# Block-sparse attention with a gated projection: some gathers put behind value products, and new schedule tables

## The chip, the cores and the metric

The kernel runs on one core of one Trainium2 chip. The metric is the device time of one execution in microseconds (us). The engines are named as the profile names them: PE (TensorE, with PEld for its weight loads), DVE (VectorE), ACT (ScalarE), POOL (GpSimd) and SP (SyncE, which here only issues DMAs).

## The reference

```python
def _attn_ref(q, k, v, sampled_blocks):          # q, k, v: (4, 8, 768, 64); sampled_blocks: (24, 3)
    scores = scale * np.matmul(q, k.transpose(0, 1, 3, 2))
    ...
    mask = np.abs(blk_i - blk_j) <= window       # blocks of 32 rows, window 1
    mask = mask | (blk_i == 0) | (blk_j == 0) | (blk_i == n_blocks - 1) | (blk_j == n_blocks - 1)
    for qb in range(n_blocks):
        for kb in sampled_blocks[qb]:
            mask[qb * block:(qb + 1) * block, kb * block:(kb + 1) * block] = True
    ...                                          # softmax over the allowed keys
    return np.matmul(attn, v)

def _moe_ref(x, w_val, conv_w, w_out):           # x: (4, 768, 512)
    gate_pre[t] = sum over k < 5 of conv_w[k] * xp[t + k]      # causal convolution along the rows
    gate = 1.0 / (1.0 + np.exp(-gate_pre))
    return gate * (x @ w_val) @ w_out
```

The attention's output, heads side by side, is `x` of the second part.

## The kernel before, in words

**Units.** The 24 query blocks of a batch are worked in pairs of neighbours: 11 ordinary pairs, and one pair of the first and the last block, which see all keys (the global pair; `GLOB_AT` says at which place of the batch it comes). An ordinary pair is one unit, the global pair two, so four batches make 52 units, numbered 0 to 51 here. An ordinary unit has its keys in a tile `kg` (a ring of 4): the first and last block, its own pair, the neighbours, and three sampled blocks for each query block. Its values are in two tiles: `va` (ring of 3) by plain DMAs, and `vb` (3 buffers) by two **gathers**, indirect DMAs that GpSimd issues, one for each query block, with row numbers from `idx`.

**Steps.** The program is one loop over steps n. In step n stand, on each engine in the order of the program: loads of keys and values for units ahead, the scaling of `qc` (two units ahead), the scores `sc` of unit n (`s` for a global unit) with maxima `mx` on DVE and exponentials `pe` on ACT, the copies of keys for unit n + 2, the value products `av` of unit n - 2, the transposes `pt` of unit n - 1 with their evictions `ptr`, and `finish` of unit n - 3 (transposes `xp`, evictions `xT`). On PE the order is thus sc(n), av(n - 2), pt(n - 1), xp(n - 3). A value block is 64 matmuls of 128x65 in the trace (48 where batches 0 and 1 take `va` in one wide piece, 96 for a global unit).

**Fills.** Between the two halves of `pt`, and after them, `fill` puts pieces of the second part: `vp` (x @ w_val, 12 matmuls) or half an `op` (times w_out, 6 matmuls), as many as the table `FILLS` says for that half step. `prepare` does pieces of the weights' decoding, of the gate (`th` on DVE and ACT) and of splitting x into a high and a low part (`xh` on ACT, `xl` on POOL), by `STEPS`. After `vp`, DVE makes `y`, ACT its high part `yh`, POOL the low part `yl`; `op` needs both. No fill can run until all weights are decoded and the first rows are ready, which is in step 23. `V_AT`, `K_AT` and `WEIGHTS_AT` say when the loads of values for the global pair (`vn`), of the next batch's keys (`k`) and of weights (`wst`) are issued.

**Order.** Each engine's instructions are kept in the program's order (the helper `InOrder`, whose line all recorded instructions have in the profile, so that rows are told apart by tile). A gather waits for its `vb` buffer, which the value products of three pairs earlier read. In the kernel before, gathers are issued in `load_values`, at the head of step n, before the scaling and the copies of keys, and their buffer is free after av(n - 3), which stands in step n - 1.

Of the kernel before, what the change touches and what calls it, by code (L numbers as in the profile page):

```python
# [11 lines left out]
AF = mybir.ActivationFunctionType  # L12
ALU = mybir.AluOpType
AX = mybir.AxisListType
SP, POOL, ACT = mybir.EngineType.SP, mybir.EngineType.Pool, mybir.EngineType.Activation

B, H, S, D = 4, 8, 768, 64
BLK, NB, NR = 32, 24, 3
# [8 lines left out]
PAIRS = [(2 * p + 1, 2 * p + 2) for p in range(NP - 1)]  # L27
RING = 4
VRING = 3
GLOB_AT = (6, 3, 5, 4)  # L30
V_AT = ((3, 5, 6), (1, 1, 4), (2, 3, 6), (5, 6, 7))
K_AT = ((11, 11, 11), (6, 6, 10), (9, 10, 10), (8, 9, 9))
LAG_T, LAG_V, LAG_X = 1, 2, 3
WEIGHTS_AT = (2, 5, 5, 6, 7, 10, 11, 17)
DECODE_LAG = 2
SCALE_AHEAD = 2
COPY_AHEAD = 2
WIDE, SPLIT = 2, 4

COPY_ON = ("PPPAAA", "PPPSSS", "SSSSSS", "SSSSSS")  # L40
Q_ON = "AAAP"
OWN_ON = ("PP", "PP", "AP", "PP")
LOW_ON = "PPPPPVPP"
OPENING = 34

SP_VALUES = ((), (), (), ())
REGS = 4

FILLS = (
    "11213202124222020022203013"  # L50
    "23432111131112010111111112"
    "01021101111120110111011101"
    "11111101212001120021110201"
    "112110"
)
STEPS = (
    "22010020122222323311322110"
    "10321201212212221224323113"
    "22311202102131332232122210"
    "13342500120220021004344321"  # L60
    "212011"
)
STEPS_TAIL = 1

# [2 lines left out]
def attention_moe(ctx, tc, qb, kb, v, ve, sampled, w_val, conv_w, w_out, ident_in, slot_in, out):  # L67
# [236 lines left out]

    def block_numbers(pr, eng):

        mine = [n for n in range(2 * NR) if {"P": POOL, "A": ACT, "S": SP}[COPY_ON[pr.bt.b][n]] == eng]
        if not mine:
            return
        assert mine == list(range(mine[0], mine[0] + len(mine)))  # L310
        first = NR * PAIRS[pr.p][0] + mine[0]
        _, regs = nc.values_load_multi_w_load_instructions(
            sm[0:1, first : first + len(mine)], engines=[eng], min_val=0, max_val=NB - 1,
            skip_runtime_bounds_check_because="block numbers are drawn from [0, 24)",
        )
        for n, reg in zip(mine, regs):
            yield 5 + 4 * (n // NR) + n % NR, reg

    def load_keys(pr):
# [13 lines left out]
        for place, reg in block_numbers(pr, SP):  # L333
            sp.dma_start(pr.kg[:, place, :], kb[:, b, bass.ds(reg, 1), :].rearrange("p o x -> p (o x)"))

    def copy_keys(pr):
        if pr.glob:
            return
        bt, kt, i0 = pr.bt, pr.kg, PAIRS[pr.p][0]
        assert bt.loaded >= 3  # L340
        if pr.seq:
            numbers = {eng: list(block_numbers(pr, eng)) for eng in (POOL, ACT)}
# [4 lines left out]
        for eng, copy in ((POOL, pool.tensor_copy), (ACT, act.copy)):  # L347
# [7 lines left out]
    def load_values(pr):  # L355
        b = pr.bt.b
        if pr.glob:
            return
        if pr.p == 0 and b:
            indices(b)  # L360
        if pr.p == 0 and SP_VALUES[b]:
            block_rows(b)
        vt = va[pr.seq % VRING]
        pr.va = vt
        if pr.p < VRING:
            sp.dma_start(vt[0 : 2 * BLK, :], ve[b])
        i0 = PAIRS[pr.p][0]
        sp.dma_start(vt[64:128, :], v[b * S + i0 * BLK : b * S + (i0 + 2) * BLK, :])
        pr.vb = three.tile([128, 2, H * DV], F32, tag="vb", name="vb")
        for j, i in enumerate(PAIRS[pr.p]):  # L370
            if j in SP_VALUES[b]:
                near = i + (1 if j else -1)
                near = (b * NB + near if 0 < near < NB - 1 else B * NB) * BLK
                sp.dma_start(pr.vb[0:BLK, j, :], v[near : near + BLK, :])
                if pr.p % REGS == 0:
                    held[j] = nc.values_load_multi_w_load_instructions(
                        sv[0:1, b, j, pr.p : min(pr.p + REGS, NP - 1), :].rearrange("p i r -> p (i r)"), engines=[SP],
                        min_val=0, max_val=B * NB,
                        skip_runtime_bounds_check_because="block numbers are drawn from [0, 24)",
                    )[1]  # L380
# [19 lines left out]
    for pr in pairs:  # L400
        for e in range(2 if pr.glob else 1):
            un = Unit()
            un.pr, un.e = pr, e
            un.last = not pr.glob or e == 1
            units.append(un)

# [62 lines left out]

    def transposes(un):  # L470
        un.PT = []
        for p in un.P:
            turn[0] += 1
            pt = (bank("pt", ps_pt, "pt") if turn[0] % 2 else ps_pt.tile([128, 512], F32, tag="pt", name="pt"))
            pt = pt.rearrange("p (c s) -> p c s", c=4)
            for c in range(4):
                transpose(pt[:, c, :], p[:, 128 * c : 128 * c + 128], ident)
            t = three.tile([128, 4, 128], F32, tag="ptr", name="ptr")
            act.copy(t, pt)
            un.PT += [t[:, c, :] for c in range(4)]  # L480
            yield

    def values(un):
# [3 lines left out]
        if pr.glob:  # L487
            assert pr.bt.loaded == 6
            pr.bt.valued += 1
            for h in range(2):  # L490
                for c in range(6):
                    pt = un.PT[4 * h + c if c < 4 else 4 + 2 * h + c]
                    for hp in range(HP):
                        cols = slice(BLK * hp, BLK * hp + BLK)
                        hd = 2 * hp + h
                        matmul(
                            pr.av[cols, un.e, h, :], pt[:, cols], pr.bt.vn[:, c, hd * DV : (hd + 1) * DV],
                            start=c == 0, stop=c == 5, tile_position=(0, BLK * hp),
                        )
        else:  # L500
# [8 lines left out]
            for a, h, b, hd in slots:  # L509
                for c in range(1 if wide else 0, 2):  # L510
                    for j in range(2):
                        rows = slice(64 * b + BLK * j, 64 * b + BLK * j + BLK)
                        vt = pr.vb[:, j, :] if c else pr.va
                        matmul(
                            pr.av[rows, a, h, :], un.PT[4 * h + 2 * a + c][:, rows], vt[:, hd : hd + DV],
                            start=c == 0, stop=a + h == 2 if wide else c == 1, tile_position=(0, rows.start),
                        )
# [9 lines left out]
    def finish(pr):  # L527
        if pr.p == 0:
            if pr.bt.b >= 2:

# [10 lines left out]
        xv = xp[:, 0:2, :].rearrange("p j (c s) -> p c j s", c=CH)  # L541
        if pr.glob:
            for e, s0 in ((0, 0), (1, S - BLK)):
                act.copy(xT[:, :, o + s0 : o + s0 + BLK], xv[:, :, e, :])
        else:
            s0 = o + PAIRS[pr.p][0] * BLK
            act.copy(xT[:, :, s0 : s0 + 2 * BLK], xp[:, 0:2, :].rearrange("p a (b s) -> p (a b) s", b=2))


    class Rows:  # L550
# [190 lines left out]
    for n in range(N + LAG_X):  # L741
# [5 lines left out]
        def more_values():  # L747
            return more("values", freed(n - LAG_V - 1) + VRING, load_values)

        if n == 0:  # L750
            more_keys()
            numbers_first = {eng: list(block_numbers(pairs[0], eng)) for eng in (POOL, ACT)}
            until("scaled", 0, scale)
            indices(0)
            until("copied", 0, copy_keys)
# [17 lines left out]
        if n == 0:  # L773
            while more_keys() or more_values():
                more_values()
        if 0 <= n - LAG_V < N:
            values(units[n - LAG_V])
        if 0 <= n - LAG_T < N:
            for half, _ in enumerate(transposes(units[n - LAG_T])):
                at_half = 2 * n + min(half, 1)  # L780
# [4 lines left out]
            prepare(int(STEPS[2 * n]))  # L785
        if 0 <= n - LAG_X < N and units[n - LAG_X].last:
            pr = units[n - LAG_X].pr
            finish(pr)
# [61 lines left out]
```

## Time and profile before

| what | value |
| --- | --- |
| median of 3 runs | 396.49 us (396.42, 399.18, 396.49) |
| the profiled execution: its time, its span | 398.18 us, 396.1 us |
| PE busy | 362.1 us of the span (91%) |
| DVE, ACT, POOL busy | 240.6, 256.4, 226.9 us |
| DMA | 72.36 MB, mean 183 GB/s |

Busy time of PE holds matmuls that overlap one another and that are drawn out by late operands, so 91% isn't 91% of its peak. Columns are explained where rows stand, below.

### The profile page before, as it was taken

What the parts mean: (1) busy time and instruction counts of PE and PEld (TensorE: products, weight loads), DVE (VectorE), ACT (ScalarE), POOL (GpSimd) and SP (SyncE); (2) the same over time, 40 slices, a digit from 0 to 9 for tenths busy, and PEclk for the clock granted to TensorE, in tenths of its full rate; (3) what the DMA queues carried; (4) which work ended last, traced back from release to release, by engine and by line L of the source; (5) the groups of instructions that cost most, each with busy time, mean ns of one, the idle gap of its engine ahead of it and who ended that gap; (6) DMA issues with size and microseconds to landing.
All of it is one profiled execution on the core that took longest, in us unless ns stands there. A gap on an engine that the chain in (4) does not pass through costs nothing.

```text
span 396.1 us, 15575 instructions
## 1 busy us (share of the span) xinstructions
PE 362.1 (91%) x6308; PEld 283.6 (72%) x6308; DVE 240.6 (61%) x523; ACT 256.4 (65%) x620; POOL 226.9 (57%) x330
## 2 busy tenths in 40 slices
PE   8689878897989999899989998999999999999995
PEld 8366555664667876679567885788678867989894
DVE  4345576567699687465684962695655566734920
ACT  1856788766798676667666776676485666553521
POOL 0874754874498856735653286854862773172640
PEclk9969999999999999999999999999999999999999
DMA  7986797999636877786546375897544434001102
GB/s 231 317 287 203 220 299 226 265 268 309 177 114 194 227 224 216 241 256 193 166 132 243 91 211 150 269 305 236 137 117 149 117 94 152 28 27 54 53 28 80
DMA packets 52439, 72.36 MB, mean 183 GB/s; under 512 B 6928, under 2 KB 34448, under 8 KB 52368
## 3 DMA queue, kind: packets, MB, share of 16 engines
q1 hardware_dynamic: 44896, 47.82, 39.8%
q0 software_dynamic: 7040, 23.43, 19.6%
q8 instruction: 50, 0.82, 0.9%
q14 instruction: 21, 0.17, 0.1%
q10 hardware_dynamic: 432, 0.11, 0.1%
HBM read 65.05 MB, written 6.29 MB: 180 GB/s over the span
## 4 chain that ended last, share of the span: by engine, by line
PE 72%; ACT 8%; DVE 6%; issue 6%; DMA 4%; POOL 1%; another core or an unknown queue 1%; SPq 0%; ACTq 0%; POOLq 0%; DVEq 0%
PE vp L85 17%; PE av L85 15%; PE op L85 14%; PE pt L85 11%; PE sc L85 10%; DVE mx L85 3%; PE s L85 3%; ACT ptr L85 2%; PE xp L85 2%; DMA k<-in_k 2%; ACT pe L85 2%; DMA vb<-in_v,idx 2%; POOL yl L85 1%; ACT th L85 1%
## 5 line engine op out<-in xcount | busy, mean ns | idle before, releaser
L85 POOL DMA_INDIRECT vb<-in_v,idx x88 | 88.7, 1008 | 45.8 <-PE av L85 24.0
L85 DVE SCALAR_TENSOR_TENSOR th<-xT,cw,th 128x384 f32<-128x384 f32 x128 | 91.0, 721 | 14.9 <-ACT th L85 11.3
L85 ACT ACTIVATE pe<-sc,mx 128x256 f32<-128x256 f32 x176 | 69.2, 481 | 42.0 <-DVE mx L85 39.2
L85 DVE TENSOR_REDUCE mx<-sc 128x2 f32<-128x512 f32 x88 | 56.6, 684 | 55.3 <-PE sc L85 42.2
L85 ACT COPY ptr<-pt 128x512 f32<-128x512 f32 x112 | 64.7, 602 | 20.2 <-PE pt L85 9.5
L85 POOL TENSOR_TENSOR yl<-y,yh 128x384 fp32r<-128x384 f32 x32 | 33.5, 1050 | 69.1 <-ACT yh L85 68.8
L85 PE MATMUL sc<-kg,qc 64*32 64x256 f32 x1408 | 57.1, 388 | 3.9 <-issue 1.3
L85 POOL COPY kg<-k 128x256 f32<-128x256 f32 (+1 forms) x154 | 50.4, 367 | 9.2 <-DMA k<-in_k 9.0
L85 PEld LDWEIGHTS av<-va,ptr 128*32 128x32 f32 (+1 forms) x1056 | 33.6, 119 | 27.9 <-issue 15.1
L85 PE MATMUL op<-wo,yh 128*128 128x512 f32 x192 | 53.1, 398 | 0.1
L85 PE MATMUL vp<-xh,wv 128*128 128x384 f32 x256 | 51.8, 344 | 0.4 <-ACT ptr L85 0.4
L85 PE MATMUL pt<-ident,pe 128*128 128x128 f32 x352 | 51.4, 283 | 0.4 <-ACT rest L85 0.4
L85 PE MATMUL av<-vb,ptr 128*32 128x65 f32 x1408 | 44.6, 224 | 7.8 <-issue 7.3
L85 PE MATMUL av<-va,ptr 128*32 128x65 f32 (+1 forms) x1056 | 45.4, 228 | 6.9 <-issue 4.1
L85 PEld LDWEIGHTS vp<-xh,wv 128*128 128x128 f32 x256 | 43.8, 188 | 0.9 <-ACT ptr L85 0.7
L85 PEld LDWEIGHTS pt<-ident,pe 128*128 128x128 f32 x352 | 39.1, 142 | 6.8 <-ACT rest L85 1.0
L85 POOL TENSOR_TENSOR xl<-xT,xh 128x384 fp32r<-128x384 f32 x32 | 35.4, 1114 | 12.7 <-ACT xh L85 12.5
L85 PEld LDWEIGHTS av<-vb,ptr 128*32 128x32 f32 x1408 | 33.6, 111 | 12.0 <-issue 9.8
L85 PEld LDWEIGHTS sc<-kg,qc 64*32 64x32 f32 x1408 | 25.8, 107 | 22.0 <-issue 13.4
L85 PEld LDWEIGHTS op<-wo,yh 128*128 128x128 f32 x192 | 35.0, 188 | 7.2 <-ACT yh L85 0.5
L85 PE MATMUL op<-wo,yl 128*128 128x512 f32 x96 | 31.8, 410 | 0.9 <-POOL yl L85 0.7
L85 ACT CAST yh<-y 128x384 fp32r<-128x384 f32 x32 | 16.8, 526 | 20.5 <-DVE y L85 17.0
(72 smaller groups left out, 461.5 us busy)
## 6 DMA issues: line engine op xcount, KB each, us to landing
kg<-in_k SPq DMA_DIRECT2D x165, 64.0 KB
vn<-in_v SPq DMA_DIRECT2D x12, 520.0 KB
qc<-in_q SPq DMA_DIRECT2D x48, 128.0 KB
k<-in_k SPq DMA_DIRECT2D x12, 512.0 KB
out<-ot SPq DMA_DIRECT2D x24, 256.0 KB
va<-in_v SPq DMA_DIRECT2D x44, 130.0 KB
wst<-in_w_val SPq DMA_DIRECT2D x4, 512.0 KB
wst<-in_w_out SPq DMA_DIRECT2D x4, 512.0 KB
```

The lines of the kernel that those rows point to most:

```text
L85: made = getattr(self.eng, name)(*args, **kwargs)
```

## The change

The gathers are no longer issued in `load_values`: they are put on a list `waiting`, and `gather` issues all that is on it. A letter for each step in the new table `GATHER` says where. S: at the head of the step, as before (also steps 0 to 2). U: after av(n - 2) in POOL's order, with no wait of its own. G: there too, and the gather waits until the last matmul of av(n - 2) has ended (`un.done`). W: the values of one pair more are loaded behind av(n - 2), with no added wait. Of 56 letters 25 are S, 24 G, 5 U and 2 W; G stands at steps 4 to 8, 10, 15, 18, 26 to 28, 31 to 36, 38 to 41 and 53 to 55, U at 1 to 3, 17 and 37, W at 43 and 44. The steps that follow a global pair by three and four have no gather to issue in either kernel.

Other parts: `Q_ON` moves the scaling of `qc` in batch 2 from ACT and in batch 3 from POOL to DVE (12 each). `PTR_ON` and `XT_ON` move 7 of 112 `ptr` evictions and 7 of 52 `xT` evictions from ACT to DVE. `LOW_ON` moves one weight chunk's low part from DVE to POOL and another the other way. `OPENING` is 31 matmuls instead of 34. The global pair of batch 1 comes one place later. `FILLS` and `STEPS` have new numbers throughout.

`OWN_ON` names DVE for some of a pair's own keys. It is read as `OWN_ON[b]` in `copy_keys`, where `b` is not the pair's batch but the enclosing function's last loop value, 3, in both kernels; its entry is "PP" before and after, so in the built programs POOL copies these keys in both, and DVE has no `kg` copy in either.

```diff
-GLOB_AT = (6, 3, 5, 4)
-V_AT = ((3, 5, 6), (1, 1, 4), (2, 3, 6), (5, 6, 7))
-K_AT = ((11, 11, 11), (6, 6, 10), (9, 10, 10), (8, 9, 9))
+GLOB_AT = (6, 4, 5, 4)
+V_AT = ((2, 5, 8), (0, 0, 7), (0, 0, 4), (3, 5, 6))
+K_AT = ((10, 11, 11), (7, 8, 11), (3, 8, 11), (3, 4, 9))
-WEIGHTS_AT = (2, 5, 5, 6, 7, 10, 11, 17)
+WEIGHTS_AT = (0, 5, 5, 5, 5, 7, 12, 15)
-Q_ON = "AAAP"
-OWN_ON = ("PP", "PP", "AP", "PP")
-LOW_ON = "PPPPPVPP"
-OPENING = 34
+Q_ON = "AAVV"
+OWN_ON = ("VP", "DP", "AD", "PP")
+LOW_ON = "PVPPPPPP"
+OPENING = 31
...
+GATHER = "SUUUGGGGGSGSSSSGSUGSSSSSSSGGGSSGGGGGGUGGGGSWWSSSSSSSSGGG"
...
-    "11213202124222020022203013"
...
+    "34010041212004102202401223"
...
         for e, dst, of in ((0, kt[:, 2:4, :], bt.k[:, i0 : i0 + 2, :]), (1, kt[:, 4:9:4, :], bt.k[:, i0 - 1 : i0 + 3 : 3, :])):
-            {"P": pool.tensor_copy, "V": dve.tensor_copy, "A": act.copy}[OWN_ON[b][e]](dst, of)
+            {"P": pool.tensor_copy, "V": dve.tensor_copy, "A": act.copy, "D": one_by_one}[OWN_ON[b][e]](dst, of)
...
-            pool.indirect_dma_start(
-                out=pr.vb[:, j, :], out_offset=None, in_=v,
-                in_offset=bass.IndirectOffsetOnAxis(ap=idx[:, b, i : i + 1], axis=0),
+            waiting.append((pr.vb[:, j, :], idx[:, b, i : i + 1]))
+
+    waiting = []
+
+    def gather(behind=None):
+
+        while waiting:
+            rows, numbers = waiting.pop(0)
+            made = pool.indirect_dma_start(
+                out=rows, out_offset=None, in_=v, in_offset=bass.IndirectOffsetOnAxis(ap=numbers, axis=0)
             )
+            if behind is not None:
+                tc.add_manual_dep(
+                    made.ins, behind.ins.name,
+                    mybir.DependencyInfo(mybir.DependencyClass.Sync, mybir.DependencyReason.DATA),
+                    reason="gathers behind the value products",
+                )
...
-            act.copy(t, pt)
+            (act.copy if PTR_ON[2 * un.n + min(half, 1)] == "A" else dve.tensor_copy)(t, pt)
...
+        if GATHER[n] == "S" or n < LAG_V:
+            gather()
...
         if 0 <= n - LAG_V < N:
             values(units[n - LAG_V])
+            if GATHER[n] == "W":
+                while more("values", freed(n - LAG_V) + VRING, load_values):
+                    pass
+            gather(units[n - LAG_V].done if GATHER[n] == "G" else None)
```

**POOL in steps 37 and 38**, before. The gathers of `vb` stand at the head of each step, `qc` and the two copies into `kg` behind them, then the step's `yl` and `xl`:

```order
L85 DMA vb<-in_v,idx 128x520 x2
L85 TENSOR_SCALAR qc<-qc 128x256
L85 COPY kg_161<-k 128x256
L85 COPY kg_161<-k 128x2x128
L85 TENSOR_TENSOR yl<-y,yh 128x384
L85 TENSOR_TENSOR xl<-xT,xh 128x384
L85 TENSOR_TENSOR yl<-y,yh 128x384
L85 TENSOR_TENSOR xl<-xT,xh 128x384
L85 DMA vb<-in_v,idx 128x520 x2
L85 TENSOR_SCALAR qc<-qc 128x256
L85 COPY kg_162<-k 128x256
L85 COPY kg_162<-k 128x2x128
```

The same steps in the change, behind the last row of step 36 (the ring of `kg` is numbered from 157 instead of 160):

```order
L88 TENSOR_TENSOR xl<-xT,xh 128x384
L88 COPY kg_158<-k 128x256
L88 COPY kg_158<-k 128x2x128
L88 DMA vb<-in_v,idx 128x520 x2
L88 COPY kg_159<-k 128x256
L88 COPY kg_159<-k 128x2x128
L88 DMA vb<-in_v,idx 128x520 x2
```

The copies now stand ahead of the gathers, `qc` is gone from POOL, and the `yl` and `xl` of these steps have gone to other steps.

**DVE where batch 2's first row numbers (`idx`) are made**, before:

```order
L85 TENSOR_TENSOR x<-av,rs 128x256
L85 SCALAR_TENSOR_TENSOR y<-th,vp 128x384
L85 SCALAR_TENSOR_TENSOR th<-xT,cw,th 128x384 x4
L85 TENSOR_SCALAR row<-base 128x24
L85 TENSOR_TENSOR row<-row,valid 128x24
L85 TENSOR_SCALAR idx<-row 128x24
L85 TENSOR_REDUCE mx<-sc 128x2 x2
```

The same place in the change:

```order
L88 TENSOR_TENSOR x<-av,rs 128x256
L88 SCALAR_TENSOR_TENSOR th<-xT,cw,th 128x384 x3
L88 COPY ptr<-pt 128x512
L88 TENSOR_SCALAR row<-base 128x24
L88 TENSOR_TENSOR row<-row,valid 128x24
L88 TENSOR_SCALAR idx<-row 128x24
L88 TENSOR_SCALAR qc<-qc 128x256
L88 TENSOR_REDUCE mx<-sc 128x2 x2
```

An eviction and a scaling have come in, the scaling just ahead of the maxima.

**SP at the program's start**, before (`va` is a pair's values, `vn` the values for the global pair, 520 KB a piece):

```order
L85 DMA va_164<-in_v 64x520
L85 DMA qc<-in_q 128x256 x2
L85 DMA vn<-in_v 128x2x520
L85 DMA va_165<-in_ve 64x520
L85 DMA va_165<-in_v 64x520
L85 DMA va_166<-in_ve 64x520
L85 DMA va_166<-in_v 64x520
L85 DMA qc<-in_q 128x256 x2
L85 DMA vn<-in_v 128x2x520
L85 DMA qc<-in_q 128x256
L85 DMA vn<-in_v 128x2x520
L85 DMA wst<-in_w_val 128x1024
```

The same in the change:

```order
L88 DMA va_161<-in_v 64x520
L88 DMA wst<-in_w_val 128x1024
L88 DMA qc<-in_q 128x256
L88 DMA vn<-in_v 128x2x520
L88 DMA qc<-in_q 128x256
L88 DMA va_162<-in_ve 64x520
L88 DMA va_162<-in_v 64x520
L88 DMA va_163<-in_ve 64x520
L88 DMA va_163<-in_v 64x520
L88 DMA qc<-in_q 128x256 x2
L88 DMA vn<-in_v 128x2x520
L88 DMA qc<-in_q 128x256 x2
```

The first weight chunk (512 KB) now stands ahead of all `vn`, and the third `vn` comes two steps later, behind the rows shown.

## Rows read from the trace of the kernel before

**Rows 1.** The page's second part: 40 slices, PE's granted clock and DMA, in tenths.

```profile
PEclk9969999999999999999999999999999999999999
DMA  7986797999636877786546375897544434001102
```

**Rows 2.** Stretches: length; busy of PE, PEld, DVE, ACT, POOL; clock, DMA share, GB/s.

```profile
24.98:129.63 104.65, 91.44 (x2070) 63.28 (x2070) 72.55 (x165) 79.91 (x206) 67.64 (x118) 0.98 0.75 226
129.63:332.83 203.20, 192.34 (x3514) 153.24 (x3521) 127.83 (x264) 136.79 (x322) 123.70 (x157) 1.00 0.64 188
332.83:396.00 63.17, 59.12 (x506) 51.98 (x506) 30.38 (x52) 26.76 (x56) 21.58 (x20) 1.00 0.13 49
```

**Rows 3.** TensorE's waits from 130 to 340: waited for, total, times, longest.

```profile
PE av L85 <- issue: 8.6, 22, 0.5
PE op L85 <- POOL yl L85: 0.7, 2, 0.4
```

**Rows 4.** Busy time of av alone in two stretches; the second is one undisturbed block.

```profile
128.00:345.00 217.00, 46.05 (x2060) 36.54 (x2048) 17.34 (x60) 1.00 0.61 181
170.00:176.00 6.00, 1.14 (x64) 0.98 (x64) 0.57 (x2) 1.00 0.91 263
```

**Rows 5.** The chain that ended last, units 38 and 39: start, us, what.

```profile
241.00 0.35 PE av L85 x13
...
241.90 0.48 issue
...
244.00 1.02 PE pt L85 x8
...
247.66 1.07 PE av L85 x64
```

**Rows 6.** POOL's timeline in the same units; brackets: idle before, and its releaser.

```profile
240.32 1.03 POOL L85 DMA_INDIRECT vb<-in_v,idx  x1 [0.16 <-issue]
241.66 0.95 POOL L85 DMA_INDIRECT vb<-in_v,idx  x1 [0.30 <-issue]
...
248.43 1.04 POOL L85 DMA_INDIRECT vb<-in_v,idx  x1 [0.15 <-issue]
```

**Rows 7.** The chain: a gap in unit 9, and sc of unit 15.

```profile
61.87 1.22 issue
...
86.96 1.37 PE sc L85 x21
...
89.55 0.38 issue
...
92.00 1.22 PE av L85 x48
```

**Rows 8.** POOL's gathers at unit 15: first and last of four.

```profile
85.63 0.97 POOL L85 DMA_INDIRECT vb<-in_v,idx  x1 [0.16 <-issue]
...
89.41 1.05 POOL L85 DMA_INDIRECT vb<-in_v,idx  x1 [0.30 <-issue]
```

**Rows 9.** The chain at the start and in unit 37.

```profile
13.99 6.91 DMA vb<-in_v,idx
...
238.18 1.03 POOL yl L85
```

**Rows 10.** Groups with shapes apart: busy us, mean ns, idle before.

```profile
L85 POOL TENSOR_SCALAR qc<-qc 128x256 f32<-128x256 f32 x12 | 11.0, 913 | 0.2
...
L85 DVE TENSOR_SCALAR words<-wst 128x512 f32<-128x512 f32 x8 | 4.6, 579 | 0.0
...
L85 DVE TENSOR_SCALAR row<-base 128x24 f32<-128x24 f32 x4 | 1.9, 470 | 0.0
```

**Rows 11.** Timeline at 79 us, DVE and POOL.

```profile
79.16 1.36 DVE L85 TENSOR_SCALAR row<-base 128x24 f32<-128x24 f32 x1
79.23 1.26 POOL L85 TENSOR_TENSOR wo<-words,wo 128x512 fp32r<-128x512 f32 x1
```

**Rows 12.** POOL's timeline in the last batch: a gather at the queue's head.

```profile
306.89 1.02 POOL L85 DMA_INDIRECT vb<-in_v,idx  x1 [7.53 <-PE av L85]
```

More of the change, by code (lines that the diff above doesn't have):

```diff
@@ L14 @@
 AX = mybir.AxisListType
-SP, POOL, ACT = mybir.EngineType.SP, mybir.EngineType.Pool, mybir.EngineType.Activation
+SP, POOL, ACT, DVE = (mybir.EngineType.SP, mybir.EngineType.Pool, mybir.EngineType.Activation, mybir.EngineType.DVE)
 B, H, S, D = 4, 8, 768, 64
@@ L40 @@
 COPY_ON = ("PPPAAA", "PPPSSS", "SSSSSS", "SSSSSS")
-Q_ON = "AAAP"
-OWN_ON = ("PP", "PP", "AP", "PP")
-LOW_ON = "PPPPPVPP"
-OPENING = 34
+Q_ON = "AAVV"
+OWN_ON = ("VP", "DP", "AD", "PP")
+LOW_ON = "PVPPPPPP"
+OPENING = 31
+PTR_ON = "AAAAAAAAAVAAAAAAAAAAAAAAAAAAAAAAAAAAAAAAAAAAAVAAAVAAAAAAAAAAAAAAAAAAAAVAVAAAAAAVAAAAAAVAAAAAAAAAAAAAAAAA"
+XT_ON = "AAAAAAAAAAVAAAAAAAAAAAAAVAAAAAAAAAAAAAAAAAAVVAVAVAVA"
+GATHER = "SUUUGGGGGSGSSSSGSUGSSSSSSSGGGSSGGGGGGUGGGGSWWSSSSSSSSGGG"
 SP_VALUES = ((), (), (), ())
@@ L49 @@
 FILLS = (
-    "11213202124222020022203013"
[L51 to L54, printed above, removed]
+    "34010041212004102202401223"
+    "01112031012352003423141201"
+    "12011101111120113011101011"
+    "11011112112101020101130101"
+    "220005"
 )
 STEPS = (
[L57 to L61, printed above, removed]
+    "10210122012222223311221222"
+    "11302202121202202142330634"
+    "22211312100450041008011244"
+    "10332402010330301011020330"
+    "011000"
 )
@@ L305, in block_numbers @@
     def block_numbers(pr, eng):
-        mine = [n for n in range(2 * NR) if {"P": POOL, "A": ACT, "S": SP}[COPY_ON[pr.bt.b][n]] == eng]
+        mine = [n for n in range(2 * NR) if {"P": POOL, "A": ACT, "S": SP, "V": DVE}[COPY_ON[pr.bt.b][n]] == eng]
         if not mine:
@@ L334, in load_keys, with one_by_one @@
             sp.dma_start(pr.kg[:, place, :], kb[:, b, bass.ds(reg, 1), :].rearrange("p o x -> p (o x)"))
+    junk = const.tile([128, 1], F32, name="junk")
+    def one_by_one(dst, of):
+        dve.tensor_scalar(out=dst, in0=of, scalar1=1.0, scalar2=None, op0=ALU.mult, op1=ALU.add, accum_out=junk)
     def copy_keys(pr):
@@ L341, in copy_keys @@
         if pr.seq:
-            numbers = {eng: list(block_numbers(pr, eng)) for eng in (POOL, ACT)}
+            numbers = {eng: list(block_numbers(pr, eng)) for eng in (POOL, ACT, DVE)}
         else:
@@ L345, in copy_keys @@
         for e, dst, of in ((0, kt[:, 2:4, :], bt.k[:, i0 : i0 + 2, :]), (1, kt[:, 4:9:4, :], bt.k[:, i0 - 1 : i0 + 3 : 3, :])):
-            {"P": pool.tensor_copy, "V": dve.tensor_copy, "A": act.copy}[OWN_ON[b][e]](dst, of)
-        for eng, copy in ((POOL, pool.tensor_copy), (ACT, act.copy)):
+            {"P": pool.tensor_copy, "V": dve.tensor_copy, "A": act.copy, "D": one_by_one}[OWN_ON[b][e]](dst, of)
+        for eng, copy in ((POOL, pool.tensor_copy), (ACT, act.copy), (DVE, one_by_one)):
             for place, reg in numbers[eng]:
@@ L402, in attention_moe @@
             un = Unit()
-            un.pr, un.e = pr, e
+            un.pr, un.e, un.n = pr, e, len(units)
             un.last = not pr.glob or e == 1
@@ L471, in transposes @@
         un.PT = []
-        for p in un.P:
+        for half, p in enumerate(un.P):
             turn[0] += 1
@@ L495, in values @@
                         hd = 2 * hp + h
-                        matmul(
+                        un.done = matmul(
                             pr.av[cols, un.e, h, :], pt[:, cols], pr.bt.vn[:, c, hd * DV : (hd + 1) * DV],
@@ L513, in values @@
                         vt = pr.vb[:, j, :] if c else pr.va
-                        matmul(
+                        un.done = matmul(
                             pr.av[rows, a, h, :], un.PT[4 * h + 2 * a + c][:, rows], vt[:, hd : hd + DV],
@@ L525, in values, with finish @@
             )
-    def finish(pr):
+    def finish(pr, n):
+        copy = act.copy if XT_ON[n] == "A" else dve.tensor_copy
         if pr.p == 0:
@@ L543, in finish @@
             for e, s0 in ((0, 0), (1, S - BLK)):
-                act.copy(xT[:, :, o + s0 : o + s0 + BLK], xv[:, :, e, :])
+                copy(xT[:, :, o + s0 : o + s0 + BLK], xv[:, :, e, :])
         else:
             s0 = o + PAIRS[pr.p][0] * BLK
-            act.copy(xT[:, :, s0 : s0 + 2 * BLK], xp[:, 0:2, :].rearrange("p a (b s) -> p (a b) s", b=2))
+            copy(xT[:, :, s0 : s0 + 2 * BLK], xp[:, 0:2, :].rearrange("p a (b s) -> p (a b) s", b=2))
     class Rows:
@@ L751, in attention_moe @@
             more_keys()
-            numbers_first = {eng: list(block_numbers(pairs[0], eng)) for eng in (POOL, ACT)}
+            numbers_first = {eng: list(block_numbers(pairs[0], eng)) for eng in (POOL, ACT, DVE)}
             until("scaled", 0, scale)
@@ L775, in attention_moe @@
                 more_values()
+            gather()
         if 0 <= n - LAG_V < N:
             values(units[n - LAG_V])
+            if GATHER[n] == "W":
+                while more("values", freed(n - LAG_V) + VRING, load_values):
+                    pass
+            gather(units[n - LAG_V].done if GATHER[n] == "G" else None)
         if 0 <= n - LAG_T < N:
@@ L787, in attention_moe @@
             pr = units[n - LAG_X].pr
-            finish(pr)
+            finish(pr, n - LAG_X)
             pr.bt.done.add(pr.p)
```

## The prediction

> **What bounds the kernel now.** I read the slices first. PE has its full clock but for one slice early on, and DMA is heavy in the first half above all [rows 1]. Then I cut the span at steps. Units 3 to 22 (the first row) take 104.7 us, 5.2 a unit, with PE, ACT, DVE and POOL between 65 and 87% busy; there is nothing to fill with yet. Units 23 to 50, with the second part as filling, take 203.2 us with PE busy for 192.3, and the tail is PE alone [rows 2]. So from unit 23 on only PE time counts, and the question is how much of it isn't work.
>
> TensorE's waits in that stretch hardly name another engine. 0.7 us falls to POOL's yl. The largest group is "issue" in the value products av: 22 gaps, 8.6 us [rows 3]. Busy time says the same: av is busy for 46.05 us with 2060 matmuls, while one undisturbed block of 64 takes 1.14 [rows 4]. 2060 x 1.14 / 64 is 36.7, so av loses 46.05 + 8.6 - 36.7 = 17.9 us. That is most of what this stretch loses.
>
> The chain shows where. In step 38 av runs from 241.00 to 244.00 with gaps of up to 0.48; in step 39 it takes its 1.07 [rows 5]. POOL's timeline beside it: in step 38 two gathers run from 240.32 to 242.6, through that block; in step 39 the gather starts at 248.43, when the block is all but over [rows 6]. Read like this, from the start of av to that of pt, eleven blocks are drawn out by 0.6 to 2.3 us, 16.4 together: those of steps 25, 26, 27, 32, 33, 38, 40, 44, 48, 49 and 50. Gathers run in or right ahead of each of them. The other 20 blocks are within 0.5 us of their least, mostly with the gathers beside pt, vp or op. Gathers cost PE time if they fall on the many small instructions, and next to none beside large matmuls. Why PE gets no instruction then, the trace doesn't say.
>
> The Trainium skill (Runtime: NRT & Kernel Launch, "Instruction fetch mechanics") says that a sequencer refills its instructions by DMA a page ahead, and that the cost of a page boundary is mostly hidden. By it these gaps would not hang on what POOL does, and the time would stay near 396. The rows speak against that, though they don't settle it (first rival).
>
> Before step 23 it's less clean. In step 15 four gathers in a row [rows 8] go with an sc that takes from 86.96 to 92.00, some 5 us, with gaps. But there is also a gap of 1.22 in step 9, with no gather near it [rows 7].
>
> **The change part by part.** The sum is made against the profiled 398.18 us (span 396.1 and 2.1 around it); the median of the runs is 396.49, a factor of 0.9958.
>
> Gathers behind av, from unit 23 on. Of the eleven blocks seven are in steps with a G or W now (26, 27, 32, 33, 38, 40, 44): 1.9, 2.0, 1.7, 2.3, 1.9, 0.9 and 1.4, together 12.1 us. A G gather cannot start before its av has ended. A pair of gathers takes 2.3 us (240.32 to 242.61 [rows 6]), and from the end of av (244.00) to the next av (247.66) there are 3.7 us even in a step with only half an op as filling [rows 5], so they fit unless POOL comes late. I take 11 (bounds 0, if the gaps don't hang on gathers, and 12.1). The other four (25, 48 to 50, 4.3 us) keep S. There POOL ran late, with qc scalings of 0.913 us behind the gathers of each step [rows 10]; these go to DVE, 11.0 us less on POOL, so that an S gather starts nearer to the end of the av that frees its buffer. I take 2 (0 to 4.3).
>
> Units 3 to 22. G stands at 4 to 8, 10, 15 and 18. There sc, s and av lose, read as above, 2.1, 3.1 and 4.0 us in steps 5, 7 and 15, with gathers on them; step 15's is [rows 7]. Without filling there is little more than pt between av and the next sc, 1.02 us [rows 5] for 2.3 us of gathers, so about half of the overlap moves to sc. I take 4 (a gain of 9.2 to a loss of 4, eight G steps at 0.5).
>
> The added wait. What is queued behind a waiting gather on POOL is the yl and xl of the step, and op on PE waits for yl; yl ended on the chain in unit 37 [rows 9]. Eight G steps have op pieces in the new order (26, 31, 32, 34 to 36, 38, 41). With yl ready at once and POOL in the gathers, each could lose 2.3 us, 18 together; at zero, yl comes from ACT later than the gathers end. PE lost only 0.7 on yl before [rows 3], with the gathers ahead of yl too, so I stay near the low end: 3 lost.
>
> Scaling on DVE. 24 scalings, at half the size of a 128x512 one of 0.579 us: 0.29 each, 7 us. But row<-base, four small ones, means 0.470 [rows 10], and one of these took 1.36 us at 79.16 and ended as POOL's wo did [rows 11]; 24 such would be 33 us. DVE is busy for 63% of units 23 to 50 [rows 2], and mx is wanted a step later, so PE's filling hides both: 0, with 4 lost if that cover is thin in steps with one op piece, and 2 gained from 5 us less on ACT. The Trainium skill (SBUF — State Buffer, "SBUF: two separate sides") speaks against this move: VectorE and GpSimd share a port pair as an exclusive lock, and an instruction of VectorE that uses both ports waits until GpSimd's ends. The row at 79.16 looks like that; by it the upper price would hold, still off PE's path.
>
> Loads. Two of batch 2's key loads came together, at place 6 of batch 1 (`K_AT`), which is step 15; they are now a step apart and later. I take 1 (3 gained to 2 lost). At the start a weight chunk of 512 KB stands ahead of the first gathers, whose landing at 20.9 us is on the chain after 6.91 us [rows 9]; the third vn is gone from there. 0, with 2.3 either way (512 KB at the 226 GB/s of units 3 to 22 [rows 2]).
>
> At nothing: the new fills (the matmuls are the same; two pieces more of op before the tail are two pieces less in it; 3 either way), 14 evictions on DVE, three opening matmuls fewer (0.8 us ahead of PE's wait for keys), the swapped weight chunks, the place of a global pair. OWN_ON is read with another b, so no key goes to DVE: nothing.
>
> Sum: -11 - 2 - 4 + 3 - 1 = -15, 383.2 against 398.18, which by the factor is 381.6. I say **382**, 3.7% faster.
>
> **The rivals.** *The gaps stay.* The gaps come from PE's own supply of instructions, or follow the gathers to pt, sc and the next av. For it: gaps without a gather [rows 7], and G in short steps. Against it: 11 blocks with and 20 without [rows 4 to 6]. Then the 17 us of the terms on gathers are mostly gone, 1 to 4 are left from POOL and loads, and yl takes them back: 392 to 399.
>
> *POOL is held.* Slower than before: the wait holds POOL until av ends, then 2.3 us of gathers, then yl, in eight steps with op, 18 us, against 13 gained from unit 23 on; with the 4 of units 3 to 22 lost instead of gained that makes 398.18 - 13 - 1 + 18 + 4, 406, and by the factor 404. It decides where yh is ready before the gathers end and op comes within 3.4 us of av's end. For it: at 306.89 a gather had held POOL's head for 7.53 us, waiting for av [rows 12]. Against it: op's first half needs no yl.
>
> *More is gained.* All gathers off av and sc, 12.1 + 4.3 + 9.2, yl costs nothing, loads 3: 369.6, by the factor 368.
>
> **How the numbers follow.** The forecast 0.66 (375 to 391), the gaps stay 0.16, POOL is held 0.08, more is gained 0.10. The range runs from 374 to 394: it leaves out most of the third rival, half of the first and the second. A measurement of this kernel can tell about 1% from no change, 4 us. Faster by over 1%: 0.66 + 0.10 + 0.05 of the first rival, 0.81; within 1% 0.11; slower 0.08.
>
> **What would show it.** Right: av in steps 26 to 44 at 1.07 (1.17 wide), the "issue" group of av after unit 23 at 3 us or less, gathers starting as av ends. Units 3 to 22 in 98 to 102 us. Wrong: gaps in sc or pt beside the gathers, PE waiting for yl by several us, or mx late on DVE behind a scaling. The forecast fails most easily where POOL comes so late that a G gather runs into the next av.

## The result, and the profile after

| kernel | median | runs |
| --- | --- | --- |
| before | 397.18 us | 396.42 to 399.18, 4 runs |
| after | 381.02 us | 379.04 to 383.33, 4 runs |

The ratio is 0.9588, with a 95% interval of 0.9521 to 0.9654: 4.1% faster. All ratios here leave out slow runs, those over 1.5% above the fastest of the same kernel, so they can differ a little from the quotient of the medians shown. The profiled execution after took 383.33 us, with a span of 381.5.

The span was cut where the changed kernel's units 3, 23 and 51 begin on PE, as in [rows 2]. Columns: stretch, its length, then busy time of PE, PEld, DVE, ACT and POOL with instruction counts, granted clock, DMA share, GB/s.

```profile
24.95:125.84 100.89, 91.37 (x2069) 64.13 (x2069) 72.12 (x167) 79.03 (x203) 73.19 (x125) 0.97 0.82 246
125.84:320.87 195.03, 190.41 (x3525) 155.70 (x3525) 134.35 (x294) 129.20 (x300) 109.76 (x139) 0.99 0.67 194
320.87:381.50 60.63, 56.10 (x489) 48.98 (x488) 32.24 (x57) 26.12 (x55) 21.62 (x20) 0.99 0.12 45
```

Against [rows 2], units 3 to 22 are 3.8 us shorter (104.65 to 100.89), units 23 to 50 8.2 (203.20 to 195.03), the tail 2.5 (63.17 to 60.63). Together 14.5 of the span's 14.6. The tail is shorter because work left it: 108 matmuls of `op` stand in it where 114 did, and 132 of `vp` where 144 did, and these are in units 23 to 50 now. The two stretches together gain 10.7 us.

Where it came from is read on the waits, from 130 to 335 us, of the changed kernel (columns as in [rows 3]); the last line is a wait on POOL that is new in size.

```profile
POOL vb L88 <- PE av L88: 29.5, 15, 4.0
...
PE av L88 <- issue: 3.3, 5, 1.6
...
PE av L88 <- ACT ptr L88: 0.9, 2, 0.6
```

The "issue" gaps of av are 3.3 us in 5 pieces, where [rows 3] has 8.6 in 22. No wait of `op` for `yl` is left in the list. Instead POOL's gathers sit 29.5 us for av, which is the added wait. The busy time of av alone, to be held against [rows 4]:

```profile
128.00:335.00 207.00, 38.79 (x1962) 32.38 (x1959) 16.21 (x56) 0.99 0.62 181
```

By the working of the prediction, 1962 x 1.14 / 64 is 34.9, so av loses 38.79 + 3.3 - 34.9 = 7.2 us, where it lost 17.9. Read block by block, 2.4 of these are step 42, shown below, 2.3 step 23 and 2.0 the steps 27, 29 and 39; in these last four steps there is hardly a gather on av, or none. POOL's timeline shows how, in steps 40 to 42 (brackets: idle before, and its releaser), and after it the chain that ended last, in the same steps.

```profile
250.24 0.97 POOL L88 DMA_INDIRECT vb<-in_v,idx  x1 [1.81 <-PE av L88]
251.52 1.31 POOL L88 DMA_INDIRECT vb<-in_v,idx  x1 [0.30 <-issue]
...
255.67 0.96 POOL L88 DMA_INDIRECT vb<-in_v,idx  x1 [1.80 <-PE av L88]
...
261.02 0.97 POOL L88 DMA_INDIRECT vb<-in_v,idx  x1 [0.16 <-issue]
262.30 0.95 POOL L88 DMA_INDIRECT vb<-in_v,idx  x1 [0.30 <-issue]
```

```profile
248.83 1.07 PE av L88 x64
249.90 1.02 PE pt L88 x8
...
254.26 1.07 PE av L88 x64
255.33 0.59 PE pt L88 x4
...
261.08 0.83 PE av L88 x33
261.91 0.46 issue
```

In steps 40 and 41, marked G, av takes its 1.07 us and ends at 249.90 and 255.33; the gathers start 0.34 us behind it, beside `pt` and the filling. In step 42, marked S, the gathers start at 261.02 as av does, and av breaks into pieces as in [rows 5]: read as in the prediction, from the start of av to that of `pt`, 3.5 us instead of 1.07.

### The profile page after: what moved, and what is told of

Its sections match the earlier page's. It is cut to its first block, busy times and chain, and to the rows that moved or that the text cites. A ratio compares the mean times of both kernels' runs of the same rounds, so it can differ in the third digit from the quotient of the medians.

```text
span 381.5 us, 15551 instructions
## 1 busy us (share of the span) xinstructions
PE 356.6 (93%) x6302; PEld 283.3 (74%) x6302; DVE 248.9 (65%) x561; ACT 247.3 (65%) x594; POOL 217.9 (57%) x318
## 4 chain that ended last, share of the span: by engine, by line
PE 80%; ACT 5%; DVE 4%; issue 4%; DMA 4%; POOL 1%; SPq 0%; ACTq 0%; POOLq 0%; DVEq 0%
PE vp L88 17%; PE op L88 16%; PE av L88 16%; PE pt L88 14%; PE sc L88 11%; PE s L88 3%; PE xp L88 2%; DVE mx L88 2%; DMA vb<-in_v,idx 2%; DMA k<-in_k 2%; ACT ptr L88 2%; ACT pe L88 1%; DVE th L88 1%; POOL yl L88 1%; SPq L88 0%
## 5 line engine op out<-in xcount | busy, mean ns | idle before, releaser
L88 POOL DMA_INDIRECT vb<-in_v,idx x88 | 90.8, 1032 | 68.9 <-PE av L88 43.4
L88 DVE SCALAR_TENSOR_TENSOR th<-xT,cw,th 128x384 f32<-128x384 f32 x128 | 86.1, 682 | 11.2 <-ACT th L88 7.1
L88 ACT COPY ptr<-pt 128x512 f32<-128x512 f32 x105 | 60.8, 603 | 12.8 <-PE pt L88 11.4
L88 POOL COPY kg<-k 128x256 f32<-128x256 f32 (+1 forms) x154 | 52.4, 378 | 9.4 <-DMA k<-in_k 8.8
L88 PE MATMUL av<-va,ptr 128*32 128x65 f32 (+1 forms) x1056 | 43.6, 229 | 5.0 <-ACT ptr L88 2.4
L88 PE MATMUL av<-vb,ptr 128*32 128x65 f32 x1408 | 40.9, 224 | 5.6 <-issue 5.0
L88 PEld LDWEIGHTS vp<-xh,wv 128*128 128x128 f32 x256 | 45.1, 193 | 0.2
L88 PEld LDWEIGHTS sc<-kg,qc 64*32 64x32 f32 x1408 | 26.0, 108 | 22.3 <-issue 10.1
L88 PEld LDWEIGHTS op<-wo,yh 128*128 128x128 f32 x192 | 34.9, 188 | 6.9
L88 POOL TENSOR_TENSOR xl<-xT,xh 128x384 fp32r<-128x384 f32 x32 | 33.6, 1058 | 10.3 <-ACT xh L88 10.2
L88 PEld LDWEIGHTS av<-vb,ptr 128*32 128x32 f32 x1408 | 31.3, 111 | 8.0 <-issue 5.6
L88 DVE SCALAR_TENSOR_TENSOR y<-th,vp 128x384 f32<-128x384 f32 x32 | 17.6, 551 | 21.8 <-PE vp L88 18.1
```

Source lines behind the costliest of these rows:

```text
L88: made = getattr(self.eng, name)(*args, **kwargs)
```

## The experiments

Every set of runs has its own runs of the kernel before, on the same chip, and the ratios below are to these. Four chips or more were met, and they are not alike: on one of them the kernel before takes 372.8 us, on the others 396.6 to 398.5. So the ratio is what counts, and a ratio only tells of chips of its kind.

| run | what it is | median, us | before there | ratio, 95% interval |
| --- | --- | --- | --- | --- |
| e1_gathers_alone | gathers moved, old tables | 379.36 | 372.76 | 1.0191 (1.0097 to 1.0285) |
| e2_at_head | change, all gathers at the head | 376.25 | 372.76 | 1.0107 (1.0015 to 1.0199) |
| e3_no_wait | change, no added wait | 379.59 | 372.76 | 1.0179 (1.0053 to 1.0305) |
| e4_on_products | change, gathers put on av | 373.92 | 372.76 | 1.0023 (0.9986 to 1.0061) |
| r1_change | the change | 379.45 | 397.69 | 0.9516 (0.9449 to 0.9583) |
| r2_before | the kernel before, for its trace | 397.50 | 397.69 | one run |
| e6_own_keys | change, own keys really on DVE | 384.21 | 397.69 | 0.9645 (0.9580 to 0.9711) |
| e8_old_fills | change, old `FILLS` and `STEPS` | 394.21 | 397.69 | 0.9899 (0.9834 to 0.9963) |
| g1_at_head | as e2 | 386.53 | 396.60 | 0.9729 (0.9675 to 0.9783) |
| g2_on_products | as e4 | 405.02 | 396.60 | 1.0190 (1.0134 to 1.0246) |
| g3_no_wait | as e3 | 393.36 | 398.46 | 0.9876 (0.9808 to 0.9943) |
| g4_step42 | change, G at step 42 too | 381.27 | 398.46 | 0.9547 (0.9485 to 0.9609) |

The theory was the prediction's: gathers on the value products cost TensorE time, and the change takes them off. The main rival: the gaps are TensorE's own and fall where they fall.

### Four edits on a chip of the other kind

**e1_gathers_alone**: the `GATHER` table and its waits stay; the other tables, the engines of the evictions among them, are those of before.

```diff
-Q_ON = "AAVV"
+Q_ON = "AAAP"
...
-    "34010041212004102202401223"
+    "11213202124222020022203013"
```

> The kernel before with all its own tables, engines and loads; only the table GATHER and its waits are taken from the change. Theory (gathers that run on GpSimd beside the value products stall TensorE; standing behind them they don't): most of the gain is here, 383 to 388 us. Rival (the new fills, loads and engine choices make the gain, the placement is incidental): 394 to 398 us.

**e2_at_head**:

```diff
-GATHER = "SUUUGGGGGSGSSSSGSUGSSSSSSSGGGSSGGGGGGUGGGGSWWSSSSSSSSGGG"
+GATHER = "SSSSSSSSSSSSSSSSSSSSSSSSSSSSSSSSSSSSSSSSSSSSSSSSSSSSSSSS"
```

> The changed kernel with S in every step: gathers at the head of the step as before, all else as changed. Theory: the value products after unit 23 lose 10 to 16 us again, 391 to 397 us. Rival: the gain stays, 379 to 385 us.

**e3_no_wait**: each G becomes U, the same place in POOL's order without the wait.

```diff
-GATHER = "SUUUGGGGGSGSSSSGSUGSSSSSSSGGGSSGGGGGGUGGGGSWWSSSSSSSSGGG"
+GATHER = "SUUUUUUUUSUSSSSUSUUSSSSSSSUUUSSUUUUUUUUUUUSWWSSSSSSSSUUU"
```

> The changed kernel with U for each G: the gathers keep their place in GpSimd's order, without the wait for the value products of the step. Theory: where GpSimd comes early a gather starts when its buffer is free, right behind the value products of the step before, and where it comes late it falls on those of this step; some of the stalls return, 383 to 389 us. Rival: the wait does nothing, 379 to 383 us.

**e4_on_products**: each G becomes A, and an A gather is issued behind the last score matmul of its step, so that it starts as av does.

```diff
         if n < N:
             scores(units[n])
+            if GATHER[n] == "A":
+                gather(units[n].scored)
```

> The changed kernel with each G gather made to wait for the last score matmul of the step instead, so that it starts with the value products. Theory: 11 such steps after unit 23 lose 1.2 to 2.3 us each (13 to 25 us) and the 8 before it some, 396 to 412 us. Rival: within 4 us of the change, 378 to 385 us.

All four came within 2% of the kernel before, with the one that puts gathers on av the fastest, and as absolute times the expectations are of no use, since the kernel before takes 24 us less there. The busy time of av in e4_on_products shows why nothing is told apart (second line: one block, that of step 31, with a gather on 0.99 us of it):

```profile
128.00:345.00 217.00, 38.59 (x1984) 32.75 (x1984) 16.22 (x57) 1.00 0.59 173
187.99:189.46 1.47, 1.47 (x64) 1.25 (x64) 0.00 (x0) 1.00 0.50 140
```

1984 x 1.14 / 64 is 35.3, so av loses 3.3 us though 11 blocks have a gather on them; av has no "issue" gap in its list of waits. On this chip gathers cost a block 0.5 us at the most. What the theory says is cheap there, so these runs speak neither for nor against it on the chip of the main comparison. They suggest that the gain isn't to be had on every chip, but they don't show it: the change itself was not run on this one, and its ratio there stays open.

### The change and the kernel before once more

**r1_change** and **r2_before** have no edit.

> The change itself, unaltered, on another day's chip. On the chip of the first four experiments the kernel before took 372.8 us where the main comparison had 397.2, and there the value products were hardly drawn out beside gathers (0.6 us of excess over 9 blocks with all gathers at the head, where the kernel before lost 16.4 over 11 on the chip of the main comparison). Theory: what the change removes is a stall of TensorE's supply beside gathers that one chip has and the other hardly. Then, if the kernel before takes about 373 here, the change is at a ratio of 0.99 to 1.02 to it; if it takes about 397, at 0.95 to 0.97. Rival: the new tables are worth their gain on any chip, and the first four experiments lost because each undid a part that matters; then 0.95 to 0.97 where the kernel before takes 373 too.

> The kernel before, unaltered, for its trace on this chip. Theory: if it takes about 373 us, the eleven blocks of value products with gathers after unit 23 lose 3 us or less together, against 16.4 on the chip of the main comparison, and no register move of SyncE takes over 0.05 us (there, 11 of 167 took over 0.08, up to 0.46). If it takes about 397, both are as they were. Rival: the value products are drawn out as before, over 10 us, and the 24 us lie elsewhere, in transfers that land sooner or in units 3 to 22.

This set fell on a chip of the first kind. The change is at 0.9516, the theory's case for such a chip; the rival wasn't tested, since that needed the other chip. The second trace of the kernel before repeats the first: its waits (130 to 335 us) and the busy time of av are

```profile
PE av L85 <- issue: 8.5, 20, 0.5
```

```profile
128.00:345.00 217.00, 45.91 (x2032) 36.46 (x2032) 17.41 (x60) 1.00 0.61 179
```

Read as in the prediction, ten of its eleven blocks of av lose 16.4 us (the block of step 25 has no gather on it this time, and is whole), and the other twenty-one about 1. In the change on the same chip one block loses 2.4 and the 29 others from step 24 on lose 2.4 together. Units 3 to 22 are 2.7 us shorter than before (102.9 to 100.2). That is no more than one program differs by from trace to trace: g4_step42, below, has the change's program up to there and takes 102.8.

### Where the gathers stand, on chips like the first

**g1_at_head** and **g2_on_products** are e2 and e4 once more.

> The change with every gather at the head of its step (as e2), for a chip on which the kernel before takes about 397 us. Theory: the gathers' place behind the value products is what the new tables live on, and with them at the head eight to eleven blocks of value products are drawn out again: 390 to 397 us, a ratio of 0.98 to 1.00, with value products after unit 23 losing over 10 us. Rival: the new fills alone bring it, since the old fills took back 15 of the change's 18 us: 379 to 385, a ratio of 0.95 to 0.97. Where the kernel before takes about 373, neither is tested, and this is at 1.00 to 1.02 as e2 was.

> The change with the gathers of its G steps issued behind the last score matmul, so that they run on the value products (as e4), for a chip on which the kernel before takes about 397 us. Theory: each block of value products with gathers on it loses 1 to 2 us: of 16 such steps after unit 23 some 10 are hit, so 10 to 25 us more than the change, 390 to 405, with value products after unit 23 losing over 10 us and no other tile much. Rival: the gaps are TensorE's own and fall where they fall: 379 to 385, value products no worse than in the change. Where the kernel before takes about 373, neither is tested, and this is at 1.00 as e4 was.

The same edit that cost nothing on the other chip now makes the kernel 1.9% slower than before, at the upper end of the theory, and about 25 us slower than the change. In g2_on_products step 31 shows it on the chain that ended last; then POOL's gathers, and the busy time of that block:

```profile
189.22 0.83 PE av L88 x47
...
190.48 0.41 issue
190.89 0.27 PE av L88 x2
191.16 0.46 issue
...
193.00 1.05 PE pt L88 x4
```

```profile
189.59 0.97 POOL L88 DMA_INDIRECT vb<-in_v,idx  x1 [1.63 <-PE s L88]
190.87 0.95 POOL L88 DMA_INDIRECT vb<-in_v,idx  x1 [0.31 <-issue]
```

```profile
189.15:192.93 3.78, 2.37 (x64) 1.57 (x64) 0.00 (x0) 0.95 0.50 140
```

47 matmuls go in 0.83 us, then, with the gather running, a few at a time with gaps of 0.4. The block takes 3.78 us; the same block of the same kernel took 1.47 on the other chip. Ten blocks lose 21.7 us for 17.0 us of gathers on them, the 18 others up to 345 us lose 0.7. This is what the theory asks: the gaps went where the gathers were put. The rival that they are TensorE's own is out for these chips. But it isn't all of the 25 us, and here the theory fell short: from unit 23 on av takes 17.6 us more than in r1_change, and pt, vp and op together 8.8 more. A lower clock goes with that (last section).

g1_at_head is at 0.9729, between the two expectations: six blocks lose 9.4 us, not eight to eleven. So the place of the gathers is worth 1.4 to 2.1% (0.9729 against 0.9588 and 0.9516), 6 to 8 us, and the rest of the gain is there with every gather at the head. From step 24 on, blocks of av lose 10.1 us in g1, 4.8 in r1_change and 16.9 in r2_before.

### The fills

**e8_old_fills**:

```diff
-    "34010041212004102202401223"
+    "11213202124222020022203013"
...
-    "10210122012222223311221222"
+    "22010020122222323311322110"
```

> The change with the two tables of filling pieces of the kernel before. Theory: the matmuls are the same and the fills were put at nothing, within 3 us either way of the change run beside it; the place of the gathers fits the new fills no better than the old. Rival: the new fills go with the waits (op pieces put where yl is late on POOL); then this is slower than the change by 6 us or more, with PE waiting for yl.

Both tables go back at once, `FILLS` and `STEPS`, so the run doesn't tell the filling from the pieces of `prepare`. The rival's number came true: 14.8 us slower than the change beside it, 0.9899 to before. Part of that stands where no filling can run yet: of the 17.6 us between this trace and r1_change's, 5.4 are there when unit 23 begins, and 12.3 come after it. TensorE's waits there, from 130 to 335 us:

```profile
PE av L88 <- issue: 4.9, 10, 1.1
...
PE op L88 <- POOL yl L88: 2.1, 4, 0.9
...
PE pt L88 <- issue: 1.5, 1, 1.5
...
PE sc L88 <- issue: 0.7, 2, 0.5
```

`op` waits 2.1 us for `yl`, as the rival had it, but that is the smaller part. Four blocks of av with gathers lose 6.3 us, seven sc with gathers 2.3. In steps 28 and 29, for one, four gathers stand in a row on POOL from 168.87 us, behind the av of step 28, and the last two run on the sc and av of step 29 (0.7 and 1.2 us lost). A gather behind av needs filling behind it, and by the old tables some steps have little. At the end it is plainest: in the change steps 47 to 49 have one piece of `op` each and take 4.73 to 4.75 us from one sc to the next, so that a pair of gathers of 2.3 us fits between av and the next sc; with the old fills step 47 has no piece and step 48 three (3.3 and 9.9 us), and the blocks of steps 48 to 50 lose 3.1 us, where they lost 3.7 in r2_before.

Put together, as ratios to before: new tables and new places 0.9516 to 0.9588, new tables with all gathers at the head 0.9729, new places with the old tables 0.9899. All of these have the change's other parts too. Neither the tables nor the places have the gain by themselves.

### The wait, and one step more

**g3_no_wait** is e3 once more. **g4_step42**:

```diff
-GATHER = "SUUUGGGGGSGSSSSGSUGSSSSSSSGGGSSGGGGGGUGGGGSWWSSSSSSSSGGG"
+GATHER = "SUUUGGGGGSGSSSSGSUGSSSSSSSGGGSSGGGGGGUGGGGGWWSSSSSSSSGGG"
```

> The change with its gathers in the same places of POOL's order, but without the wait for the value products (as e3), for a chip on which the kernel before takes about 397 us. In the change POOL's gathers idle 43 us for the value products' end, 25 times. Theory: the wait is what keeps the gathers off the value products; without it a gather starts as soon as its buffer is free and POOL gets to it, and part of the blocks are hit again: about as with all gathers at the head, 384 to 391, a ratio of 0.97 to 0.985, with 5 to 12 us lost in value products after unit 23. Rival: the place in POOL's order is enough, and the wait only holds yl back: 375 to 381, no more than 3 us lost there. Where the kernel before takes about 373, neither is tested, and this is at 1.02 as e3 was.

> The change with the wait at step 42 as well, the one step after unit 23 whose value products are still drawn out by a gather at the head (2.4 us in each of three traces). Theory: that block takes its 1.1 us, its gathers go beside the filling behind it, and the total falls by about 2 us, a ratio of 0.945 to 0.955 where the kernel before takes about 397; near what repeated runs can tell, so the trace of the step decides. Rival: the step has no room for a pair of gathers behind the products, and the same 2 us are lost in the scores or the products of step 43.

Without the wait the change is at 0.9876: two thirds of the gain and more are gone, and it takes 2 us more than the theory's upper end. In the list of waits from 130 to 335 us:

```profile
POOL vb L88 <- PE av L88: 14.3, 9, 2.6
PE av L88 <- issue: 7.5, 16, 0.9
```

The gathers wait for av 14.3 us instead of 29.5 (what is left is for their buffer), and av's gaps are back at 7.5 us; six blocks lose 11.9. The place in POOL's order is not enough, since POOL runs ahead of PE. The rival is out.

g4_step42 is at 0.9547, no gain that can be told from the change's 0.9516 or 0.9588. It lies in the theory's range, but so does 0.9516, and the trace of the step decides. The chain that ended last, in step 42:

```profile
257.95 1.15 PE av L88 x64
...
259.35 0.97 POOL vb L88
...
260.63 0.66 POOL vb L88
...
261.60 1.01 POOL yl L88
...
262.65 0.50 PE op L88
```

av is whole (1.15 us), the gathers start behind it, and `yl` stands behind the gathers on POOL; `op` waits 1.90 us for it. The step gets 9.7 us long, where it was 9.9 and 10.0 with S. So the loss only changes its name, and marking this step brings nothing that can be told: neither the theory's 2 us nor the rival's place (the next scores), but the prediction's price of the added wait.

### Own keys

**e6_own_keys**:

```diff
-            {"P": pool.tensor_copy, "V": dve.tensor_copy, "A": act.copy, "D": one_by_one}[OWN_ON[b][e]](dst, of)
+            {"P": pool.tensor_copy, "V": dve.tensor_copy, "A": act.copy, "D": one_by_one}[OWN_ON[bt.b][e]](dst, of)
```

> The change with the table of own keys read by the pair's own batch instead of the last value of an outer loop, so that VectorE (and ScalarE, twice) really copies some keys that GpSimd copies in the change as it stands. Theory: as I read the code, the copies moved by the change are none, and POOL isn't what TensorE waits for, so this is within 1% of the change run beside it. Rival: POOL's copies ahead of the gathers are what delays them; then 1% or more faster than the change, with gathers that start sooner.

DVE now has 33 copies of keys, as its rows say (duration in ns: least, median, most):

```profile
L88 DVE TENSOR_SCALAR_CACHE_REDUCE kg<-k x22: 402/409/414, 69.0 to 228.7; 128x256 f32<-128x256 f32 x22
...
L88 DVE COPY kg<-k x11: 281/285/865, 10.3 to 64.4; 128x256 f32<-128x256 f32 x11
```

By the medians it is 4.8 us slower than the change beside it, more than the theory's 1% and against the rival's sign; the two intervals just overlap, so the size isn't sure. The largest single difference is in step 19, where two gathers fall on av: 2.06 us on a block that loses 2.8, where the change has 0.35 us on it and 0.4 lost. That these gathers come to lie on av because POOL has less to do ahead of them is a reading, not shown.

## Why the prediction was right, and where its working was not

The forecast was 382 us, measured 381.02; the sum was -15 and the profiled time fell by 14.85 (398.18 to 383.33). The mechanism is shown, on chips like the first, by g2, g1 and the change: the same gathers on av, at the head, and behind av, at 1.019, 0.973 and 0.952 to 0.959. Several of the terms are nevertheless not what was written, and that the sum came so close is in part luck.

- *Gathers behind av from unit 23*, -11 (0 to 12.1). The seven blocks are clean but for 0.6 us in step 27, with no gather beside it. But the change against g1 gives only 6 to 8 us for all places. The term was too large: it counted the blocks that were hit before, and the change's other parts spare some of them with the gathers at the head too (g1 has six hit, before eleven). How the new tables, or the scalings taken off POOL, move a gather that stands at the head was not followed step by step, and stays open.
- *The four S blocks*, -2 (0 to 4.3). All four are clean in the change, 4.1 gained, close to the upper bound. The reason given, POOL free of the `qc` scalings, isn't enough: e8 has the scalings on DVE, and the blocks of steps 48 to 50 lose 3.1 us. What e8 lacks are the new tables.
- *Fills, at nothing*. This step failed. They were taken as the same matmuls in another order; they are what sets the room behind av. With the old tables 14.8 us of the gain go, some two thirds of it, by the traces, from unit 23 on. The rest is lost before any filling runs, where only `STEPS` differs, which the sum left out; whether `STEPS` or that run cost it is open. (What leaves the tail is a piece of `op` and one of `vp`, not two of `op`.) The forecast came out all the same, because the blocks that the new tables cleared had been put down to the other two terms: two errors that covered each other.
- *Units 3 to 22*, -4 (gain 9.2 to loss 4): 3.8 and 2.7 us, near the forecast. The reason isn't shown: these units take 100.9 and 100.2 us in the two traces of the change, 102.8 in g4 with the same program there, and 101.9 in g1 with every gather at the head.
- *The added wait holds yl*, +3 (0 to 18). From unit 23 on the change's lists show no such wait of `op`: 0, the lower bound. That the price is real where a step has it, g4 (1.9 us) and e8 (2.1) show; the rival *POOL is held* is that chain, and it decided one step.
- *Scaling on DVE*, 0. The 24 cost 10.2 us (row below), against 7 and 33 as the two prices, and PE's list of waits has none for `mx`. Seven took 0.40 to 1.64 us, each beside a copy or an add on POOL, and six of them end 0.15 to 0.16 us behind it; 17 took 0.27 to 0.29, several of them beside a gather. Answer to [rows 10], then one of the long ones with POOL's add beside it:

```profile
L88 DVE TENSOR_SCALAR qc<-qc 128x256 f32<-128x256 f32 x24 | 10.2, 426 | 0.0
```

```profile
299.91 1.03 POOL L88 TENSOR_TENSOR xl<-xT,xh 128x384 fp32r<-128x384 f32 x1 [2.22 <-ACT xh L88]
299.97 1.12 DVE L88 TENSOR_SCALAR qc<-qc 128x256 f32<-128x256 f32 x1
```

The Trainium skill (SBUF — State Buffer, "SBUF: two separate sides") has this as an exclusive lock between the two engines' ports; the seven agree with it. The delays were few, and their cost stayed off PE's path.

- *Own keys, nothing*: as it was; made to work, it was 1.3% slower, with intervals that overlap. *Loads*, -1: not tried alone; it lies within units 3 to 22.
- Not foreseen, and small: av now waits for evictions `ptr`, 0.9 us for ACT's (the waits above) and 0.5 for a moved one on DVE; and one gap of 1.6 us in step 23 has no gather beside it.

Of the rivals, *the gaps stay* is out on the chips like the first by g2. The Trainium skill (Runtime: NRT & Kernel Launch, "Instruction fetch mechanics"), which calls the cost of a page boundary in an engine's instructions mostly hidden, does not describe them: gaps of 0.4 us and more stand in the blocks with gathers. Nor does a load of instructions account for them: the block of step 38 in g2_on_products (250.2 to 253.8 us) has three gaps of 0.4 us, and in that time the trace has no packet of an instruction queue. What keeps TensorE from its next instruction while GpSimd issues a gather no row shows, and it stays open.

## What to carry to other kernels

When an engine shows gaps that name no releaser, lay the timeline of the others beside each gap and compare the blocks with and without; then put the suspect where it should hurt, and see whether the gaps follow. A table that places one thing and a table that places the cover for it are one edit: cost them together, because either alone may bring only part (here 1.0% and 2.7% of over 4%). Look up what stands behind a waiting instruction in its queue before marking one more place; and take the gain on more than one chip before it is called the kernel's.

## What was not expected of the hardware

Chips differ by more than the whole change. The kernel before takes 372.8 us on one and 396.6 to 398.5 on the others, at granted clocks of 0.99 on both. It was not traced on the one; the four kernels that were move the same 72.4 MB as it does. Where it takes longer, TensorE isn't the only engine that stumbles. The register moves of SyncE ahead of its key loads, in the kernel before (r2_before) and then in e4_on_products on the other chip (duration in ns: least, median, most):

```profile
L85 SPq MOVE kg<-in_k x165: 2/29/482, 59.3 to 308.8; - x165
```

```profile
L88 SPq MOVE kg<-in_k x165: 29/29/38, 58.9 to 300.6; - x165
```

In ten traces from chips of the first kind 78 of SyncE's 1670 moves took over 0.08 us, and 52 of these lie beside a gather, though only a quarter of all moves do; in four traces from the other chip none took over 0.042. It looks as if something that the engines share in taking up instructions is held while gathers are issued, on these chips and hardly on that one; that is a reading of these rows, and no run took it apart. What differs between the chips no row shows, and it stays open.

In g2_on_products the granted clock fell to the 1.2 GHz level in five short stretches between 192 and 275 us, 17 us together. Each begins at the end of a block of av with gaps or within 0.7 us behind one (steps 31, 33, 36, 38 and 40). r1_change was at 2.4 GHz in all of its units 23 to 50. The rows of the two pages, 40 slices in tenths, g2_on_products first:

```profile
PEclk9969989999999999999898989889999999999999
```

```profile
PEclk9969999999999999999999999999999999999999
```

17 us at half the clock would cost up to 8.5 us, an estimate from these stretches; pt, vp and op took 8.8 us more. So in this run the gaps seem to have cost clock besides their own time.
